# Plain float32 projections as row tiles, and the tails' products as column tiles, in an attention and feed-forward kernel on one core

## The chip, the core and the metric

The kernel runs on one core of a Trainium2 chip. The core has a matrix engine (PE; its weight loads are listed apart as PEld), a vector engine (DVE), a scalar engine (ACT), a general engine (POOL) and a queue that issues transfers (SP). The metric is the device time of one execution in microseconds (us). The time shown for a kernel is the median of several runs.

## What is computed

```
def phi(x):
    proj = x @ w_phi                                   # [64] -> [128]
    proj = proj - max(abs(proj), axis=-1, keepdims)
    return concat([exp(proj), exp(-proj)])             # 256 features
q_p, k_p = phi(q), phi(k)                              # 8 batches, 8 heads, 576 rows
kv  = k_p.T @ v ;  z = sum(k_p, rows)
x   = (q_p @ kv) / (q_p @ z + 1e-6)                    # heads side by side: 512 columns
h   = x.T @ U @ V ;  u = x + h.T                       # mixing over the 576 rows, rank 32
out = u + relu(u @ w_ch1) @ w_ch2                      # 512 -> 2048 -> 512
```

q, k, v and w_phi are float32; U, V and the two large weights come as 64-bit floats and are turned into 32-bit ones by the kernel.

## The kernel before, in words

Heads are worked on in pairs: 8 batches of 4 pairs, 32 in all (class `Pair`). Of the 576 rows of a head 512 are the main part, and the last 64 of both heads of a pair are handled together as the "tail". A pair goes through stages: `transposes`, `s_project_k0`, `s_project_k1`, `s_project_q0`, `s_kv0_q1`, `s_kv1`, `s_out0`, `s_out1`. Between two stages `pace.step()` puts a piece of the feed-forward part (class `Mixer`: `hidden`, L636, and `add`, L657) of the batch before. While one pair (`cur`) gives its outputs, the next (`nxt`) is projected, and the one after that (`far`) is loaded and transposed. When all attention is done, the feed-forward part of what is left follows alone. A scheduler then sets the order of each engine's instructions; each engine runs its own in order.

Two number formats matter. A plain float32 matmul is as exact as the data. A float32r matmul takes numbers of fewer bits; to keep the result exact the kernel splits a number into a high and a low part (`hi`, `lo`) and adds several products. The feed-forward part does so everywhere (three products for one).

The projections by w_phi (64 rows deep, while the array has 128) are done in two ways:

- Batches 0 and 1 (`split` is false): q and k are transposed by PE (L328), and the projections are plain float32 (L389 for K, L432 for Q) against `w_two`, a weight tile in which the two heads' copies of w_phi stand in a block diagonal, so that half of the product is by zeros.
- Batches 2 to 7 (`split` is true): q and k come in by 16 transfers a pair and are transposed by DVE in place (L320). ACT then writes the high parts into one half of the 128 rows of `T` (L323), and DVE the low parts into the other half (L324). So one float32r matmul of 128 rows multiplies high and low parts at once. K takes 8 matmuls of 256 columns a pair (L404), against `w_hl`, which holds the high and the low part of w_phi side by side; ACT copies one half of the result (L407) and DVE adds the other (L408). Q takes 4 matmuls of 512 columns (L427, L428).

The tails are projected in L378/L379 and L416/L417 (L381 and L419 in batches 0 and 1). The products of the features, `kv_main` (L450) and `out_main` (L491), are plain float32 and divided into two column tiles: each matmul has 64 output partitions, and two neighbours use the two halves of the array. The tails' part of kv (L441) and of the output (L477) use the whole array. In L477 both heads' kv stand side by side, and half of the product is not used.

PSUM has 8 banks here: 3 for attention and small products ("at"), 1 for the hidden layer ("ph") and 4 for its output ("o"). In batch 0 some attention tiles use "o". In the first 88 us 37 matmuls on zeros (L763, `keep_busy`) fill PE.

Of the kernel before, what the change touches and what calls it, by code (L numbers as in the profile page):

```python
# [21 lines left out]
P = 128  # L22
# [3 lines left out]
def tile_kernel(  # L26
# [60 lines left out]
    w_hl = const.tile([P, 2, F], F32R, name="w_hl")  # L87
    w_hi, w_lo = w_hl[:, 0, :], w_hl[:, 1, :]
    w_two = const.tile([P, 2, F], F32, name="w_two")

    def load_w_phi():

        for g in range(2):
            nc.sync.dma_start(out=w_f[g * D:(g + 1) * D, :], in_=w_phi)
        nc.gpsimd.memset(w_two, 0.0)
        for g in range(2):
            r_ = slice(g * D, (g + 1) * D)
            nc.vector.tensor_copy(out=w_two[r_, g, :], in_=w_f[r_, :])
        nc.vector.tensor_copy(out=w_hi, in_=w_f)
        nc.vector.tensor_sub(w_lo, w_f, f32(w_hi))  # L100
# [153 lines left out]
    class Pair:  # L254


        def __init__(self, b, j):
# [5 lines left out]
            for n, src in enumerate((k, q)):  # L263
                m = raw.tile([P, 2, SM // 2], F32, tag="raw", bufs=2, name=f"raw{nm}_{n}")
# [34 lines left out]
        def stack(self, src, dst):  # L299

            nc.scalar.copy(out=dst[0:D], in_=src)
            nc.vector.tensor_sub(dst[D:2 * D], src, f32(dst[0:D]))

        def transposes(self):
# [6 lines left out]
            dt = F32R if self.split else F32  # L311
            self.tail_T = att.tile([P, 2, P], dt, tag="tail_T", name=f"tail_T{nm}")
            if not self.split:
                nc.gpsimd.memset(self.tail_T, 0.0)
            self.T = []
            for n in range(2):
                if self.split:
                    m = att.tile([P, 2, SM], F32R, tag=f"T{n}", name=f"T{n}_{nm}")
                    x_ = self.raw[n].rearrange("p h e -> p (h e)")
                    nc.vector.transpose(out=x_, in_=x_)  # L320
                    for s in range(2):
                        here, there = (slice(i * D, (i + 1) * D) for i in (s, 1 - s))
                        nc.scalar.copy(out=m[here, s, :], in_=x_[here])  # L323
                        nc.vector.tensor_sub(m[there, s, :], x_[here], f32(m[here, s, :]))  # L324
                else:
                    pT = self.ps(f"T{n}_", True)
                    for c in range(NT):
                        nc.tensor.transpose(  # L328
                            out=pT[:, c * P:(c + 1) * P],
                            in_=self.raw[n][:, c // 2, c % 2 * P:(c % 2 + 1) * P],  # L330
                            identity=ident)
                    m = att.tile([P, SM], F32, tag=f"T{n}", name=f"T{n}_{nm}")
                    nc.scalar.copy(out=m, in_=pT)
# [3 lines left out]
                for g in range(2):  # L337
                    r_ = slice(g * D, (g + 1) * D)
                    tv = tT[r_, 0:2 * ST].rearrange("p (n r) -> p n r", n=2)
                    if self.split:  # L340
                        self.stack(tv, self.tail_T[:, :, r_])
                    else:
                        nc.scalar.copy(out=self.tail_T[r_, :, r_], in_=tv)

        def k_tile(self, n, ng):
            tag, bufs = ("feat", 3) if ng > 1 else ("feat_t", 2)
# [16 lines left out]
        def q_features(self, n, pq, m):  # L363
            nm = f"{self.nm}_{n}"
            tag, bufs = ("feat", 3) if m == SM else ("feat_t", 2)
            qp = att.tile([P, 2, m], F32, tag=tag, bufs=bufs, name=f"qp{nm}")
            nc.scalar.copy(out=qp[:, 1, :], in_=pq[:, 0:m])  # L367
# [6 lines left out]
        def project_k_tail(self):  # L374
            pk = self.ps("pkt")
            kT = self.tail_T[:, 0, :]
            if self.split:
                nc.tensor.matmul(pk[:, 0:F], kT, w_hi, start=True, stop=False)  # L378
                nc.tensor.matmul(pk[:, 0:F], kT, w_lo, start=False, stop=True)  # L379
            else:  # L380
                nc.tensor.matmul(pk[:, 0:F], kT, w_f, start=True, stop=True)  # L381
            self.kpt = self.k_features("t", pk[:, 0:F].unsqueeze(1), self.k_tile("t", 1))

        def project_k(self, g):
            if self.split:
                return self.project_k_split(g)
            pk = self.ps(f"pk{g}_", True)
            for s in range(2):
                nc.tensor.matmul(  # L389
                    pk[:, s * 2 * F:(s + 1) * 2 * F],  # L390
                    self.T[0][:, (2 * g + s) * P:(2 * g + s + 1) * P],
                    w_two.rearrange("p g f -> p (g f)"), start=True, stop=True)
            return self.k_features(
                g, pk.rearrange("p (t f) -> p t f", f=F), self.k_tile(g, NT))

        def project_k_split(self, g):

            kp = self.k_tile(g, NT)
            k_w = kp[:, :, F:2 * F]
            for s in range(2):  # L400
                pk = self.ps(f"pk{g}{s}_").rearrange("p (t n f) -> p t n f", t=2, n=2)
                for i in range(2):
                    cs = slice((2 * g + s) * P, (2 * g + s + 1) * P)
                    nc.tensor.matmul(  # L404
                        pk[:, i, :, :], self.T[0][:, i, cs], w_hl, start=True, stop=True)
                ts_ = slice(s, NT, 2)
                nc.scalar.copy(out=kp[:, ts_, 0:F], in_=pk[:, :, 1, :])  # L407
                nc.vector.tensor_tensor(  # L408
                    out=k_w[:, ts_, :], in0=pk[:, :, 0, :], in1=kp[:, ts_, 0:F], op=ALU.add)
            return self.k_features(g, k_w, kp)  # L410

        def project_q_tail(self):
            pq = self.ps("pqt")
            qT = self.tail_T[:, 1, :]
            if self.split:
                nc.tensor.matmul(pq[:, 0:2 * ST], w_hi, qT, start=True, stop=False)  # L416
                nc.tensor.matmul(pq[:, 0:2 * ST], w_lo, qT, start=False, stop=True)  # L417
            else:
                nc.tensor.matmul(pq[:, 0:2 * ST], w_f, qT, start=True, stop=True)  # L419
            self.qpt = self.q_features("t", pq, 2 * ST)  # L420

        def project_q(self, s):

            pq = self.ps(f"pq{s}_")
            if self.split:
                qT = self.T[1][:, s, :]
                nc.tensor.matmul(pq, w_hi, qT, start=True, stop=False)  # L427
                nc.tensor.matmul(pq, w_lo, qT, start=False, stop=True)  # L428
            else:
                pv = pq.rearrange("f (p z i) -> f i z p", z=2, i=2)  # L430
                for i in range(2):
                    nc.tensor.matmul(  # L432
                        pv[:, i], w_two[:, i, :],
                        self.T[1][:, s * (SM // 2):(s + 1) * (SM // 2)], start=True, stop=True)
            return self.q_features(s, pq, SM)

        def kv_tail(self):
            self.kv_ps = self.ps("kv_ps", True)
            self.kv_v = self.kv_ps[:, 0:4 * (D + 1)].rearrange("p (f h e) -> p f h e", f=2, h=2)
            for f in range(2):  # L440
                nc.tensor.matmul(  # L441
                    self.kv_v[:, f, :, :], self.kpt[:, 0, f * F:(f + 1) * F], self.vt,
                    start=(f == 0), stop=False, skip_group_check=True)

        def kv_main(self, g, kp):
            for t in range(NT):
                for f in range(2):
                    for i in range(2):
                        r_ = slice(i * H, (i + 1) * H)
                        nc.tensor.matmul(  # L450
                            self.kv_v[r_, f, g, :], kp[:, t, f * F + i * H:f * F + (i + 1) * H],
                            self.vb[:, g, t, :], start=False, stop=(t == NT - 1),
# [18 lines left out]
        def out_tail(self, xt):  # L471
# [4 lines left out]
            for f in range(2):  # L476
                nc.tensor.matmul(  # L477
# [476 lines left out]
```

## Time and profile before

| | |
|---|---|
| median of 3 runs | 1177.5 us (1177.25 to 1177.62) |
| profiled execution, its own time | 1175.22 us |
| its span | 1173.4 us |
| granted PE clock, mean | 0.999 |
| last projection of batch 1 (L432), start | 180.1 us |
| last projection of all (L427), start | 942.5 us |
| matmuls of the hidden layer and its output (L636, L657) | 3456 of 512 columns |
| transfers, mean | 86 GB/s |

A row of a group reads: line, engine, operation, output <- inputs, shape, count, then busy time in us, mean length of one in ns, the idle time of the engine just before them and what ended it. Matmuls are pipelined: one of 512 columns is listed with some 390 ns, but the next one starts earlier. So the distance between starts is what one costs, and a row of the view in order of time (start, length, line, tile, count) gives it for a run of equal ones: the whole length less the length of the last, divided by the count less one. A plain float32 matmul appears as two records, a float32r one and a transpose as one.

### The profile page before, as it was taken

To read this page: it belongs to the slowest core of one execution; us is meant where nothing else is said; L and a number is where in the kernel's file an instruction comes from. 1 tells how busy PE (TensorE), PEld (TensorE's weight loads), DVE (VectorE), ACT (ScalarE), POOL (GpSimd) and SP (SyncE) were. 2 spreads that over 40 slices of the span, in tenths; PEclk is the share of its full clock that TensorE was granted. 3 is DMA by queue.
4 is the path that set the end of the run, shared out by engine and by line. 5 is a ranking of instruction groups with operands and counts; after the bars stand their busy time and mean duration, and the time that the engine had idled before them with its cause. 6 is when DMAs were issued, how large, how long until landed. Compare 5 with 4: busy or idle time off the path is not lost.

```text
span 1173.4 us, 22343 instructions
## 1 busy us (share of the span) xinstructions
PE 1146.9 (98%) x8717; PEld 933.6 (80%) x8717; DVE 677.2 (58%) x1482; ACT 536.0 (46%) x1151; POOL 203.2 (17%) x154
## 2 busy tenths in 40 slices
PE   7989999999999999999999999999999999999998
PEld 5767877788888888788887888788878887888886
DVE  5677779766647666766657565756666533312111
ACT  5778787545534544354534444444534421111110
POOL 3344444111111121012101111112101110000000
PEclk9999999999999999999999999999999999999999
DMA  4785221421245123531353123512343026310101
GB/s 119 236 290 188 94 64 32 136 74 32 68 112 125 28 57 82 120 77 29 74 130 103 32 67 103 114 42 57 83 92 101 1 73 160 96 37 11 62 1 37
DMA packets 248307, 100.87 MB, mean 86 GB/s; under 512 B 215305, under 2 KB 227849, under 8 KB 248201
## 3 DMA queue, kind: packets, MB, share of 16 engines
q1 hardware_dynamic: 246928, 98.16, 32.0%
q8 instruction: 69, 1.13, 0.4%
q10 hardware_dynamic: 1272, 1.28, 0.4%
q14 instruction: 38, 0.30, 0.1%
HBM read 78.41 MB, written 20.97 MB: 85 GB/s over the span
## 4 chain that ended last, share of the span: by engine, by line
PE 77%; DVE 7%; DMA 5%; SPq 5%; ACT 5%; issue 1%; POOL 0%; DVEq 0%; ACTq 0%; POOLq 0%
PE ph L636 28%; PE o L657 27%; PE kv_ps L450 5%; PE xp L491 5%; SPq L622 3%; PE pk L404 2%; DMA raw<-in_q_dram 2%; PE pq L427 2%; PE pp L572 2%; SPq L270 1%; PE kv_ps L441 1%; DVE x L591 1%; DMA y<-u_dram 1%; PE xpt L477 1%; PE pq L428 1%
## 5 line engine op out<-in xcount | busy, mean ns | idle before, releaser
L636 PE MATMUL ph<-uT_hi,w 128*128 128x512 f32 x1152 | 390.3, 398 | 2.7 <-DVE h_lo L642 1.7
L657 PE MATMUL o<-w,h_hi 128*128 128x512 f32 x1152 | 321.6, 395 | 3.0 <-ACT h_hi L641 2.8
L636 PEld LDWEIGHTS ph<-uT_hi,w 128*128 128x128 f32 x1152 | 215.7, 188 | 51.2 <-DVE h_lo L642 3.3
L657 PEld LDWEIGHTS o<-w,h_hi 128*128 128x128 f32 x1152 | 211.6, 188 | 47.0 <-ACT h_hi L641 4.6
L636 PE MATMUL ph<-uT_lo,w 128*128 128x512 f32 x576 | 225.6, 392 | 0.0
L641 ACT ACTIVATE h_hi<-ph 128x512 fp32r<-128x512 f32 x144 | 85.8, 595 | 285.7 <-PE ph L636 274.6
L642 DVE SCALAR_TENSOR_TENSOR h_lo<-ph,h_hi 128x512 fp32r<-128x512 f32 x144 | 98.8, 686 | 186.9 <-ACT h_hi L641 186.3
L657 PE MATMUL o<-w,h_lo 128*128 128x512 f32 x576 | 188.4, 395 | 0.8 <-DVE h_lo L642 0.7
L368 POOL PARTITION_ALL_REDUCE qp<-qp x64 | 126.5, 1979 | 267.0 <-ACT qp L367 257.6
L657 PEld LDWEIGHTS o<-w,h_lo 128*128 128x128 f32 x576 | 105.8, 188 | 23.5 <-DVE h_lo L642 2.4
L636 PEld LDWEIGHTS ph<-uT_lo,w 128*128 128x128 f32 x576 | 108.3, 188 | 20.2 <-DVE uT_lo L249 0.2
L368 POOL PARTITION_ALL_REDUCE qp_t<-qp_t x32 | 27.4, 856 | 396.3 <-ACT qp_t L367 396.2
L450 PEld LDWEIGHTS kv_ps<-vb,kp 128*64 128x64 f32 x2048 | 69.4, 137 | 22.3 <-issue 13.5
L358 ACT ACTIVATE kp<-kp 128x512 f32<-128x512 f32 x64 | 40.4, 631 | 93.6 <-DVE kp L355 82.8
L491 PEld LDWEIGHTS xp<-kv,qp 128*64 128x64 f32 x2048 | 65.8, 137 | 21.4 <-issue 8.7
L324 DVE TENSOR_TENSOR T<-raw,T 64x512 fp32r<-64x512 f32 x96 | 69.7, 726 | 22.5 <-ACT T L323 19.9
L450 PE MATMUL kv_ps<-vb,kp 128*64 128x65 f32 x2048 | 82.4, 226 | 0.1
L491 PE MATMUL xp<-kv,qp 128*64 128x65 f32 x2048 | 76.1, 225 | 0.8 <-ACT qp L370 0.4
L323 ACT CAST T<-raw 64x512 fp32r<-64x512 f32 x96 | 59.4, 619 | 19.1 <-PE pq L428 17.8
L370 ACT ACTIVATE qp<-qp 128x512 f32<-128x512 f32 x64 | 40.4, 631 | 59.0 <-DVE qp L369 58.8
L320 DVE STREAM_TRANSPOSE raw<-raw 128x512 f32<-128x512 f32 x48 | 34.1, 711 | 55.5 <-DMA raw<-in_q_dram 29.6
L145 POOL INT64_ADD w_ab<-w_ab x32 | 43.5, 1359 | 64.2 <-DVE w_ab L141 43.6
(125 smaller groups left out, 1335.2 us busy)
## 6 DMA issues: line engine op xcount, KB each, us to landing
words<-in_moe_w_ch_dram SPq DMA_DIRECT2D x32, 512.0 KB, 8.7
w<-kept SPq DMA_DIRECT2D x30, 512.0 KB, 4.0
vb<-in_v_dram SPq DMA_DIRECT2D x64, 128.0 KB, 2.7
u_dram<-x SPq DMA_DIRECT2D x32, 256.0 KB, 2.1
st<-u_dram SPq DMA_DIRECT2D x16, 512.0 KB, 3.8
out_dram<-st SPq DMA_DIRECT2D x32, 256.0 KB, 2.3
y<-u_dram SPq DMA_DIRECT2D x112, 64.0 KB, 2.2
raw<-in_k_dram SPq DMA_DIRECT2D x192, 32.0 KB, 1.8
```

The costliest lines, as they stand in the source:

```text
L145: nc.gpsimd.int64_add(a64, a64, b64)
L323: nc.scalar.copy(out=m[here, s, :], in_=x_[here])
L324: nc.vector.tensor_sub(m[there, s, :], x_[here], f32(m[here, s, :]))
L358: nc.scalar.activation(out=kp[:, :, 0:F], in_=kp[:, :, F:2 * F], func=AF.Exp)
L368: nc.gpsimd.partition_all_reduce(qp[:, 0, :], qp[:, 1, :], P, ReduceOp.absmax)
L370: nc.scalar.activation(out=qp[:, 0, :], in_=qp[:, 1, :], func=AF.Exp)
L450: nc.tensor.matmul(self.kv_v[r_, f, g, :], kp[:, t, f * F + i * H:f * F + (i + 1) * H], self.vb[:, g, t, :], start=False, stop=(t == NT - ...
L491: nc.tensor.matmul(xv[i * H:(i + 1) * H, c, :], qp[:, f, c * P + i * H:c * P + (i + 1) * H], self.kv[:, f, c // 2 if self.split else s, :] ...
L636: nc.tensor.matmul(ph, w1_part(f, l, c), r[:, c, :], start=(n == 0), stop=(n == 3 * NCC - 1))
L641: on_act = nc.scalar.activation(out=h_hi, in_=ph, func=AF.Relu)
L642: on_dve = nc.vector.scalar_tensor_tensor(out=h_lo, in0=ph, scalar=0.0, in1=f32(h_hi), op0=ALU.max, op1=ALU.subtract)
L657: ins = nc.tensor.matmul(self.o[t], l[:, cs], w2_t[f][:, r, :], start=(f == 0 and n == 0), stop=(f == NFC - 1 and n == 2))
```

## The change

All projections become plain float32, and the difference between batches 0/1 and 2 to 7 is left to the way in which q and k are transposed. `w_two`, `w_hl` and the high and low parts of q and k are gone; the transposed tile is used as it is. Its upper 64 rows hold one head (batches 0 and 1) or one half of the rows (batches 2 to 7), its lower 64 the other. Each half is multiplied with its own copy of w_phi in the same half of `w_f`, in a matmul of 64 rows: two row tiles of the array, whose results go to two banks. `project_k` and `project_q` do both halves at once, in one stage each; `s_kv0_q1` no longer projects. The tail of K is projected one stage later. The tails' parts of kv and of the output are divided into two column tiles of 64 output partitions, as the main parts are. There is one `tail_T`, zeroed once. The raw tiles have five buffers and take the place of `T`; the features have four instead of three.

```diff
-    w_hl = const.tile([P, 2, F], F32R, name="w_hl")
-    w_two = const.tile([P, 2, F], F32, name="w_two")
+    tail_T = const.tile([P, 2, P], F32, name="tail_T")
+    nc.gpsimd.memset(tail_T, 0.0)
...
-                m = raw.tile([P, 2, SM // 2], F32, tag="raw", bufs=2, name=f"raw{nm}_{n}")
+                m = raw.tile([P, 2, SM // 2], F32, tag="raw", bufs=5, name=f"raw{nm}_{n}")
...
-                    m = att.tile([P, 2, SM], F32R, tag=f"T{n}", name=f"T{n}_{nm}")
-                    x_ = self.raw[n].rearrange("p h e -> p (h e)")
-                    nc.vector.transpose(out=x_, in_=x_)
-                    for s in range(2):
-                        here, there = (slice(i * D, (i + 1) * D) for i in (s, 1 - s))
-                        nc.scalar.copy(out=m[here, s, :], in_=x_[here])
-                        nc.vector.tensor_sub(m[there, s, :], x_[here], f32(m[here, s, :]))
+                    m = self.raw[n].rearrange("p h e -> p (h e)")
+                    nc.vector.transpose(out=m, in_=m)
...
-                    if self.split:
-                        self.stack(tv, self.tail_T[:, :, r_])
-                    else:
-                        nc.scalar.copy(out=self.tail_T[r_, :, r_], in_=tv)
+                    nc.scalar.copy(out=tail_T[r_, :, r_], in_=tv)
...
-        def q_features(self, n, pq, m):
+        def q_features(self, n, parts, m):
...
-            nc.scalar.copy(out=qp[:, 1, :], in_=pq[:, 0:m])
+            for i, part in enumerate(parts):
+                to = qp[:, 1, :]
+                if len(parts) > 1:
+                    to = to.rearrange("f (p z i) -> f i z p", z=2, i=2)[:, i]
+                nc.scalar.copy(out=to, in_=part)
...
+        def project_k(self):
+
+            pk = [self.ps(f"pk{i}_", True) for i in range(2)]
+            for c in range(NT):
+                for i in range(2):
+                    r_ = slice(i * D, (i + 1) * D)
+                    nc.tensor.matmul(
+                        pk[i][:, c * F:(c + 1) * F], self.T[0][r_, c * P:(c + 1) * P], w_f[r_],
+                        start=True, stop=True)
+            self.kp = [
+                self.k_features(
+                    i, pk[i].rearrange("p (t f) -> p t f", f=F), self.k_tile(i, NT))
+                for i in range(2)]
...
+        def project_q(self):
+
+            pq = [self.ps(f"pq{i}_") for i in range(2)]
+            for i in range(2):
+                r_ = slice(i * D, (i + 1) * D)
+                nc.tensor.matmul(pq[i], w_f[r_], self.T[1][r_, :], start=True, stop=True)
...
             for f in range(2):
-                nc.tensor.matmul(
-                    self.kv_v[:, f, :, :], self.kpt[:, 0, f * F:(f + 1) * F], self.vt,
-                    start=(f == 0), stop=False, skip_group_check=True)
...
+                for i in range(2):
+                    r_ = slice(i * H, (i + 1) * H)
+                    nc.tensor.matmul(
+                        self.kv_v[r_, f, :, :], self.kpt[:, 0, f * F + i * H:f * F + (i + 1) * H],
+                        self.vt, start=(f == 0), stop=False, skip_group_check=True)
...
             for f in range(2):
-                nc.tensor.matmul(
-                    xv, self.qpt[:, f, :], self.kv[:, f, :, :], start=(f == 0), stop=(f == 1))
+                for g in range(2):
+                    r_ = slice(g * ST, (g + 1) * ST)
+                    nc.tensor.matmul(
+                        xv[r_, g, :], self.qpt[:, f, r_], self.kv[:, f, g, :],
+                        start=(f == 0), stop=(f == 1))
...
         def s_project_k0(self):
+            self.project_k()
+
+        def s_project_k1(self):
             self.project_k_tail()
-            self.kp0 = self.project_k(0)
...
         def s_project_q0(self):
-            self.qp0 = self.project_q(0)
+            self.project_q()
 
         def s_kv0_q1(self):
             self.kv_tail()
-            self.kv_main(0, self.kp0)
-            self.qp1 = self.project_q(1)
+            self.kv_main(0, self.kp[0])
```

How this stands in PE's order is shown at two places. Names carry batch and pair (`pk00_5_0` is of batch 5, pair 0) and buffer numbers; `ph` and `o` are the feed-forward part. The first place is the K projection of batch 5, pair 0. PE before:

```order
L636 MATMUL ph3_9_6554<-uT_hi3_5483,w1_9_1929 128x512
L378 MATMUL pkt5_0_6596<-w_hl_88,tail_T5_0_6479 128x128
L379 MATMUL pkt5_0_6596<-w_hl_88,tail_T5_0_6479 128x128
L404 MATMUL pk00_5_0_6606<-w_hl_88,T0_5_0_6480 128x256 x2
L657 MATMUL o3_0_5882<-w2_8_3_5898,h_hi3_8_6471 128x512 x2
L657 MATMUL o3_0_5882<-w2_8_3_5898,h_lo3_8_6472 128x512
L657 MATMUL o3_1_5883<-w2_8_3_5898,h_hi3_8_6471 128x512 x2
L404 MATMUL pk01_5_0_6611<-w_hl_88,T0_5_0_6480 128x256 x2
```

PE now, at the same place (L596 and L617 are the hidden layer and its output in the new numbering, `pk0` the upper row tile and `pk1` the lower):

```order
L596 MATMUL ph3_9_6306<-uT_hi3_5304,w1_9_1969 128x512
L365 MATMUL pk0_5_0_6348<-w_f_87,raw5_0_0_6055 128x128
L365 MATMUL pk1_5_0_6349<-w_f_87,raw5_0_0_6055 128x128
L365 MATMUL pk0_5_0_6348<-w_f_87,raw5_0_0_6055 128x128
L365 MATMUL pk1_5_0_6349<-w_f_87,raw5_0_0_6055 128x128
L365 MATMUL pk0_5_0_6348<-w_f_87,raw5_0_0_6055 128x128
L365 MATMUL pk1_5_0_6349<-w_f_87,raw5_0_0_6055 128x128
L365 MATMUL pk0_5_0_6348<-w_f_87,raw5_0_0_6055 128x128
L365 MATMUL pk1_5_0_6349<-w_f_87,raw5_0_0_6055 128x128
L617 MATMUL o3_0_5680<-w2_8_3_5696,h_hi3_8_6243 128x512 x2
```

The four blocks of two whole-array matmuls (two of them shown) have become one block of eight row tiles, upper and lower in turn. The second place is the output of the tail (`xpt`) of batch 4, pair 3. PE before:

```order
L657 MATMUL o3_3_5885<-w2_9_1978,h_hi3_9_6567 128x512 x2
L477 MATMUL xpt4_3_6635<-kv4_3_6552,qp4_3_t_6393 128x130 x2
L636 MATMUL ph3_10_6667<-uT_hi3_5483,w1_10_2005 128x512
L636 MATMUL ph3_10_6667<-uT_lo3_5484,w1_10_2005 128x512
L636 MATMUL ph3_10_6667<-uT_hi3_5483,w1_10_2005 128x512
L491 MATMUL xp0_4_3_6646<-kv4_3_6552,qp4_3_0_6452 64x65 x16
```

PE now:

```order
L617 MATMUL o3_3_5683<-w2_9_2011,h_lo3_9_6320 128x512
L438 MATMUL xpt4_3_6384<-kv4_3_6304,qp4_3_t_6158 64x65 x4
L617 MATMUL o3_0_5680<-w2_9_2011,h_hi3_9_6319 128x512
L596 MATMUL ph3_10_6418<-uT_hi3_5304,w1_10_2038 128x512
L596 MATMUL ph3_10_6418<-uT_lo3_5305,w1_10_2038 128x512
L596 MATMUL ph3_10_6418<-uT_hi3_5304,w1_10_2038 128x512 x2
```

Two whole-array matmuls have become four column tiles, which stand alone between whole-array matmuls; the next column tiles of this pair (`xp0`) follow nine matmuls later in the new order.

More of the change, by code (lines that the diff above doesn't have):

```diff
@@ L94, in load_w_phi @@
             nc.sync.dma_start(out=w_f[g * D:(g + 1) * D, :], in_=w_phi)
[L95 to L100, printed above, removed]
     vts, vbs = [], []
@@ L297, in load_v @@
                     out=self.vt[g * D:(g + 1) * D, g, 0:D], in_=v[self.b, self.h0 + g, SM:S, :])
-        def stack(self, src, dst):
-            nc.scalar.copy(out=dst[0:D], in_=src)
-            nc.vector.tensor_sub(dst[D:2 * D], src, f32(dst[0:D]))
         def transposes(self):
@@ L310, in transposes @@
             nc.tensor.transpose(out=tT[:, 0:2 * ST], in_=self.t_r, identity=ident)
[L311 to L314, printed above, removed]
             self.T = []
@@ L331, in transposes @@
                             identity=ident)
-                    m = att.tile([P, SM], F32, tag=f"T{n}", name=f"T{n}_{nm}")
+                    m = raw.tile([P, SM], F32, tag="raw", bufs=5, name=f"T{n}_{nm}")
                     nc.scalar.copy(out=m, in_=pT)
@@ L375, in project_k_tail @@
             pk = self.ps("pkt")
-            kT = self.tail_T[:, 0, :]
+            nc.tensor.matmul(pk[:, 0:F], tail_T[:, 0, :], w_f, start=True, stop=True)
+            self.kpt = self.k_features("t", pk[:, 0:F].unsqueeze(1), self.k_tile("t", 1))
+        def project_k(self):
[10 more added lines that the diff above has]
+                for i in range(2)]
@@ L377, in project_k_tail, with project_q_tail @@
+        def project_q_tail(self):
+            pq = self.ps("pqt")[:, 0:2 * ST]
+            nc.tensor.matmul(pq, w_f, tail_T[:, 1, :], start=True, stop=True)
+            self.qpt = self.q_features("t", [pq], 2 * ST)
+        def project_q(self):
[3 more added lines that the diff above has]
+                nc.tensor.matmul(pq[i], w_f[r_], self.T[1][r_, :], start=True, stop=True)
             if self.split:
-                nc.tensor.matmul(pk[:, 0:F], kT, w_hi, start=True, stop=False)
@@ L379, in project_k_tail @@
-                nc.tensor.matmul(pk[:, 0:F], kT, w_lo, start=False, stop=True)
-            else:
[L381 to L435, printed above, removed]
+                parts = [[a] for a in pq]
+            else:
+                parts = [
+                    [a[:, g * 2 * P:(g + 1) * 2 * P].rearrange("f (z p) -> f z p", z=2) for a in pq]
+                    for g in range(2)]
@@ L437, in kv_tail @@
+            self.qp = [self.q_features(i, parts[i], SM) for i in range(2)]
         def kv_tail(self):
@@ L440, in kv_tail, with kv_main @@
             for f in range(2):
-                nc.tensor.matmul(
-                    self.kv_v[:, f, :, :], self.kpt[:, 0, f * F:(f + 1) * F], self.vt,
-                    start=(f == 0), stop=False, skip_group_check=True)
-        def kv_main(self, g, kp):
-            for t in range(NT):
+                for i in range(2):
[3 more added lines that the diff above has]
+                        self.vt, start=(f == 0), stop=False, skip_group_check=True)
+        def kv_main(self, n, kp):
+            for c in range(NT):
+                g, z = divmod(c, 2)
+                t = 2 * n + z if self.split else 2 * z + n
                 for f in range(2):
@@ L450, in kv_main @@
                         nc.tensor.matmul(
-                            self.kv_v[r_, f, g, :], kp[:, t, f * F + i * H:f * F + (i + 1) * H],
-                            self.vb[:, g, t, :], start=False, stop=(t == NT - 1),
+                            self.kv_v[r_, f, g, :], kp[:, c, f * F + i * H:f * F + (i + 1) * H],
+                            self.vb[:, g, t, :], start=False, stop=(n == 1 and z == 1),
                             skip_group_check=True)
```

14 lines of the change are left out of this document (5 added, 9 removed).

## The prediction

> **What bounds the kernel now.** First the shares of the page, then the stretches (busy us of each engine, then clock and DMA), then what TensorE waited for (total us, times, longest).
>
> ```profile
> PE 1146.9 (98%) x8717; PEld 933.6 (80%) x8717; DVE 677.2 (58%) x1482; ACT 536.0 (46%) x1151; POOL 203.2 (17%) x154
> ...
> 0.00:100.00 100.00, 86.69 (x938) 65.78 (x939) 68.58 (x177) 71.28 (x158) 38.81 (x47) 1.00 0.72 230
> 100.00:200.00 100.00, 97.13 (x745) 78.60 (x744) 78.54 (x156) 83.65 (x163) 48.56 (x34) 1.00 0.26 70
> 200.00:950.00 750.00, 744.77 (x6029) 609.83 (x6029) 477.62 (x1062) 351.57 (x779) 115.82 (x74) 1.00 0.32 77
> ...
> PE o L657 <- ACT h_hi L641: 2.8, 4, 1.0
> ...
> PE ph L636 <- DVE h_lo L642: 1.7, 3, 0.9
> ```
>
> From 200 to 950 us PE is busy 744.77 of 750 us at a clock of 1.00, while DVE and ACT are busy 64% and 47%. PE's longest waits for them in the whole span are 2.8 and 1.7 us. A busy PE need not be a PE at its peak, because matmuls overlap; so I price it by the distance between starts. The next rows are PE's order of time (start, length, line, tile, count).
>
> ```profile
> 607.97 0.64 PE L404 MATMUL pk<-w_hl,T 128*128 128x256 f32 x4
> 608.44 0.61 PE L477 MATMUL xpt<-kv,qp_t 128*128 128x130 f32 x4
> 608.81 2.08 PE L657 MATMUL o<-w,h_hi 128*128 128x512 f32 x8
> ...
> 613.44 0.61 PE L657 MATMUL o<-w,h_lo 128*128 128x512 f32 x2
> 613.99 1.15 PE L491 MATMUL xp<-kv,qp 128*64 128x65 f32 x32
> 615.07 0.73 PE L657 MATMUL o<-w,h_lo 128*128 128x512 f32 x2
> 615.64 0.64 PE L404 MATMUL pk<-w_hl,T 128*128 128x256 f32 x4
> ...
> L404 PE MATMUL pk<-w_hl,T 128*128 128x256 f32 x192 | 36.4, 291 | 0.4 <-DVE kp L408 0.4
> L427 PE MATMUL pq<-T,w_hl 128*128 128x512 f32 x48 | 23.7, 493 | 0.0
> L428 PE MATMUL pq<-T,w_hl 128*128 128x512 f32 x48 | 19.0, 396 | 0.0
> L477 PE MATMUL xpt<-kv,qp_t 128*128 128x130 f32 x128 | 19.6, 275 | 0.0
> L491 PE MATMUL xp<-kv,qp 128*64 128x65 f32 x2048 | 76.1, 225 | 0.8 <-ACT qp L370 0.4
> ```
>
> Two L657 in 0.61 us, one lasting 0.39, start 0.22 to 0.23 us apart: 0.227 for 512 columns of float32r. A 256-column one takes 0.12 (four in 0.64, the last 0.28). A plain float32 matmul shows as two records (L477: 128 records of 64 matmuls), of 0.112 each for 130 columns. The 32 records of L491, two column tiles side by side, need 0.93 us from first to last start, in 15 steps of two: 0.059 a step, but 0.10 for the first. So **plain float32 costs four times a float32r pass, and tiles side by side halve that**.
>
> The second reading is **what a change of tiling costs**. Between the starts of L657 at 613.44 and L404 at 615.64 lie 2.20 us. Four L657 take 0.91 and 16 steps of 0.059 take 0.94; 0.35 us are left. Going in, the first L491 starts 0.09 later than a 512-column matmul needs (0.32 behind the second L657 of 613.44), and its first step is 0.05 too long. Coming out, L657 starts 0.09 late (0.15 behind the last L491), and the next one 0.11 late (0.73 - 0.39 = 0.34 apart). The weight loads say why.
>
> ```profile
> 652.73 0.19 PEld L636 LDWEIGHTS ph<-uT_hi,w 128*128 128x128 f32 x1
> 652.95 0.39 PE L636 MATMUL ph<-uT_hi,w 128*128 128x512 f32 x1
> 653.27 1.01 PEld L491 LDWEIGHTS xp<-kv,qp 128*64 128x64 f32 x32 [0.35 <-issue]
> 653.27 1.15 PE L491 MATMUL xp<-kv,qp 128*64 128x65 f32 x32
> 654.35 0.19 PEld L427 LDWEIGHTS pq<-T,w_hl 128*128 128x128 f32 x1
> ```
>
> Within one tiling the load runs 0.22 ahead of its matmul. At the change it waits until the last matmul is out and then lies open: 0.05 us for 64 columns, 0.11 for 128. I take 0.14 us for a change into column tiles and 0.207 for one back to the whole array. The Trainium skill (TensorEngine Tiling (Array Packing), Key Properties) says that changing the tiling mode drains the TensorE; these rows agree for column tiles, and nothing here shows row tiles. By that rule the row tiles below pay as the column tiles do.
>
> **The change part by part.** Batches 2 to 7 have 24 head pairs, batches 0 and 1 have 8. "Late" is what lies behind the last projection of batch 1 (180 us here), "early" what lies before.
>
> ```profile
> 164.17 1.03 PE L389 MATMUL pk<-w_two,T 128*128 128x256 f32 x4
> ...
> 170.90 1.02 PE L432 MATMUL pq<-T,w_two 128*128 128x256 f32 x4
> ...
> 604.11 0.22 PE L378 MATMUL pkt<-w_hl,tail_T 128*128 128x128 f32 x1
> 604.17 0.28 PE L379 MATMUL pkt<-w_hl,tail_T 128*128 128x128 f32 x1
> 604.28 0.45 PE L636 MATMUL ph<-uT_hi,w 128*128 128x512 f32 x1
> 604.57 0.39 PE L636 MATMUL ph<-uT_lo,w 128*128 128x512 f32 x1
> ```
>
> - *K, late.* Out: 192 x 0.12 = 23.0 us. In: 192 plain float32 row tiles of 128 columns, 384 records, 192 steps of two. A step is not in the trace. Side by side it is near one record of L477, 0.112 to 0.12; one after the other it is 0.224. I take 0.115, since column tiles do run two at a time: 22.1. In the new order five of the 24 blocks are cut after an odd matmul, and the two at the cut run alone (+0.23 a block). Together +0.2.
> - *Q, late.* Out: 96 x 0.23 = 22.1. In: two row tiles of 512 columns a pair. L389 shows 0.216 a record for 256 columns (1.03 less 0.38, over 3), so 0.432 for 512 and 0.864 for the two steps; 24 times is 20.7 (41.4 one after the other). -1.4.
> - *K and Q of batches 0 and 1.* L389 and L432 are 128 records of 0.216: 27.6 us. In: 8 pairs x (0.92 + 0.864) = 14.3, and five Q pairs that the new order separates cost 0.864 more each, 4.3. -9.
> - *Tails.* k and q tails were two float32r matmuls each and become one plain float32: from 604.11 to 604.57 lie 0.46, of which L636 explains 0.227, so 0.23 as before against 2 x 0.112. Nothing. The tails' output goes from four records of 0.112 to four steps of 0.059: -0.21 x 24 late (-5.1), -1.7 early. The tails' kv part does equal work, with some cut pairs: +1.9 late.
> - *Changes of tiling.* Counted over PE's whole order, from one matmul to the next, there are 334 before and 464 now. Late, before: 121 in, 121 out, 121 x 0.347 = 42.0 us. Now 136 into columns x 0.14, 155 back to the whole array x 0.207 and 53 into rows x 0.20 (0.09 of drain and a 128-column load of 0.11): 61.8. **+19.8 late.** Row tiles are not in the trace; the nearest rows are those of the column tiles, and I let both pay alike. Early 46 x 0.347 = 16.0 becomes 47 x 0.14 + 51 x 0.207 + 22 x 0.20 = 21.5: +5.5. Row tiles bounded from both sides: if their changes are free, late has 136 x 0.347 = 47.2 (+5.2) and early 16.3; if both loads lie open one behind the other, 53 x 0.11 more, +5.8.
> - *DVE and ACT.* They lose the groups below. PE waits so little for them that I count 2 us as gained, at most the 5.2 us that PE stood idle from 200 to 950.
>
> ```profile
> L324 DVE TENSOR_TENSOR T<-raw,T 64x512 fp32r<-64x512 f32 x96 | 69.7, 726 | 22.5 <-ACT T L323 19.9
> L408 DVE TENSOR_TENSOR kp<-pk,kp 128x256 f32<-128x256 f32 x96 | 37.6, 409 | 9.2 <-ACT kp L407 9.1
> L323 ACT CAST T<-raw 64x512 fp32r<-64x512 f32 x96 | 59.4, 619 | 19.1 <-PE pq L428 17.8
> L407 ACT COPY kp<-pk 128x256 f32<-128x256 f32 x96 | 33.1, 371 | 28.8 <-PE pk L404 28.4
> ```
>
> - *Banks and buffers.* A K or Q projection now takes two of the three attention banks at once instead of one. What would wait behind it on PE is the next attention matmul and, in order, everything else. With DVE and ACT lighter I cost it at nothing; a wait of 0.2 us in each of 24 pairs would be 5 us. Five "raw" buffers replace two raw and two T buffers; the loads start no later.
>
> Sum: late 0.2 - 1.4 - 5.1 + 1.9 + 19.8 = +15.4. Early -9 - 1.7 + 5.5 = -5.2; but PE is busy only 86.69 of the first 100 us, so part of that becomes waiting, and I take -3. With -2 for shorter waits: **+10.4 us**. The profiled execution took 1175.22 us (span 1173.4), so 1185.6; the median of the runs lies 2.3 higher, 1177.5, hence **1188 us**.
>
> **The rivals.**
> 1. *Row tiles change over without a drain* (faster). The loads of rows 0 to 63 might be placed while a whole-array matmul runs out. For it: the trace shows the drain for column tiles only. Late then costs 5.2 in place of 19.8 and early 0.3 in place of 5.5. From +10.4 go 20, of which some 2 are lost in early waiting: -7.6, 1170. It decides the sign from about half of that: when a row change costs under 0.1 us.
> 2. *Row tiles share a weight path.* K changes its weights for every 128 columns. If two 128-column loads (0.11 each) go one after the other, a step is 0.22 and not 0.115: 256 steps x 0.105 = +27 us, 1215. Against it: 64-column loads of two column tiles do fit into a step of 0.059. The Trainium skill (TensorE: Matmul & The Clock Gate, Measured speedup vs the span model) has four row tiles gain 3.07 and not 4; as an estimate from that page, two tiles at 77% make the 57 us of projections 74, so 1205.
> 3. *The row tiles do not run side by side at all*, so the change does not do what it says. Late +41.6, early +10: 1240. Column tiles running two at a time speak against it.
>
> **How the numbers follow.** Forecast 0.52 (1180 to 1196), rival 1 0.25, rival 2 0.14, rival 3 0.09. The range leaves out rival 3 and thin ends: 1166 to 1217. A measurement tells 0.2% from no change, 2.4 us: rival 1 gives 0.21 faster and 0.03 same, the forecast 0.03 faster, 0.09 same and 0.40 slower, the others slower. That is 0.24, 0.12, 0.64. The forecast's own range stands beside it because both signs have weight.
>
> **What would show it.** In the new trace a K block between two whole-array matmuls should take 0.92 us beside 0.40 of changing; the starts of its records should come in twos 0.115 us apart. A Q block should take 0.86, twos 0.43 apart. The first weight load of a block should lie 0.09 us behind the drained matmul. Starts evenly 0.11 apart (16 of them, 1.8 us) mean rival 3; twos 0.22 apart rival 2; a row block that begins with no gap rival 1. DVE should lose some 120 us and ACT some 90 with no gain in the span. What would make the forecast wrong elsewhere: PE idle that names a projection bank, or many more us of PE idle between 50 and 100 us than the 13 us that the first 100 us show.

## The result, and the profile after

The changed kernel takes **1198.2 us** (median of 4 runs, 1197.4 to 1200.29) against 1177.55 us of before on the same chip. The ratio is 1.0179, with a 95% interval of 1.0161 to 1.0196: slower by about 21 us. The prediction said slower, 1188 us, with a range from 1166 to 1217. The sign holds, but the loss is twice the +10.4 us of the forecast, and 1198.2 lies above the 1180 to 1196 that the prediction gave for the forecast itself. The profiled execution took 1200.29 us, its span 1198.5.

The first row is the share of each engine on the page of after. DVE lost 106 us and ACT 77, and the span grew.

```profile
PE 1162.2 (97%) x9197; PEld 907.4 (76%) x9197; DVE 571.6 (48%) x1238; ACT 459.1 (38%) x975; POOL 200.9 (17%) x146
```

The stretches of after (start and end, length, then busy us of PE, PEld, DVE, ACT and POOL, then the granted clock, the DMA share and GB/s):

```profile
0.00:100.00 100.00, 81.92 (x938) 55.84 (x939) 60.68 (x160) 70.09 (x160) 35.76 (x39) 0.97 0.67 210
100.00:200.00 100.00, 97.49 (x819) 75.74 (x821) 75.26 (x150) 82.68 (x161) 47.35 (x33) 0.97 0.34 94
200.00:950.00 750.00, 740.34 (x6189) 576.77 (x6187) 372.93 (x815) 267.72 (x586) 113.22 (x72) 1.00 0.32 75
```

PE stood idle for 9.7 us between 200 and 950 where before had 5.2, and for 18.1 us in the first 100 where before had 13.3. The clock, 1.00 in the same three stretches of before, is 0.97 in the first two. What PE waited for in after (total us, times, longest):

```profile
PE o L617 <- ACT h_hi L601: 6.7, 5, 2.4
PE pkt L356 <- DMA w_f<-in_w_phi_dram: 5.5, 1, 5.5
...
PE pq L383 <- DVE kp_t L331: 1.9, 1, 1.9
...
PE T L307 <- ACT qp L347: 1.8, 1, 1.8
PE T L307 <- DVE kp L331: 1.7, 1, 1.7
```

L617 is before's L657, the output of the hidden layer. Its wait for ACT was 2.8 us in four pieces in before, the longest 1.0 us.

Now the row tiles themselves, in after's order of time, a K block and a Q block late in the kernel:

```profile
687.41 0.39 PE L596 MATMUL ph<-uT_hi,w 128*128 128x512 f32 x1
687.72 0.97 PEld L365 LDWEIGHTS pk<-w_f,raw 64*128 64x128 f32 x16 [0.35 <-issue]
687.72 1.16 PE L365 MATMUL pk<-w_f,raw 64*128 64x128 f32 x16
...
688.82 0.45 PE L438 MATMUL xpt<-kv,qp_t 128*64 128x65 f32 x8
...
702.96 1.13 PE L383 MATMUL pq<-raw,w_f 64*128 64x512 f32 x4
...
704.02 0.19 PEld L596 LDWEIGHTS ph<-uT_lo,w 128*128 128x128 f32 x1 [0.76 <-issue]
```

From 687.41 to 688.82 lie 1.41 us. L596 needs 0.227 of them; the 16 records start in twos, and 8 steps of 0.112 need 0.90; 0.28 is left for changing: the 0.20 going in, of drain and open load, and the 0.09 of drain coming out. The first weight load starts with the first matmul, 0.31 behind the L596 ahead of it, so 0.09 after that one is out. The Q block takes 1.06 us to the next load: two steps of 0.43, and 0.20 for its own open load and the drain coming out. **The row tiles run side by side, and a change into them costs what the forecast took.** The rivals are out: no free change, no step of 0.22, no 16 single steps. And the whole order of after has 464 changes of tiling, as counted; priced at 0.14, 0.20 and 0.207 they make 83.1 us against 57.9 for the 334 of before, +25.2 where the forecast had 19.8 + 5.5.

So the error is not in the matmuls. It is in two other terms, the waits and the early stage. The experiments divide the loss.

### The profile page after: what moved, and what is told of

The parts are those of the page before. It is cut to its first block, busy times and chain, and to the rows that moved or that the text cites. A ratio compares the mean times of both kernels' runs of the same rounds, so it can differ in the third digit from the quotient of the medians.

```text
span 1198.5 us, 22826 instructions
## 1 busy us (share of the span) xinstructions
PE 1162.2 (97%) x9197; PEld 907.4 (76%) x9197; DVE 571.6 (48%) x1238; ACT 459.1 (38%) x975; POOL 200.9 (17%) x146
## 4 chain that ended last, share of the span: by engine, by line
PE 80%; DMA 5%; SPq 4%; DVE 4%; ACT 4%; issue 2%; POOL 0%; ACTq 0%; DVEq 0%; POOLq 0%
PE ph L596 30%; PE o L617 29%; PE kv_ps L409 5%; PE xp L453 5%; PE pq L383 3%; PE pk L365 2%; SPq L582 2%; SPq L263 2%; PE kv_ps L398 2%; PE pp L532 2%; DMA u_dram<-x 1%; DMA v_st<-in_moe_V_dram 1%; PE vp L550 1%; DMA y<-u_dram 1%; ACT uT_hi L241 1%
## 5 line engine op out<-in xcount | busy, mean ns | idle before, releaser
L596 PE MATMUL ph<-uT_hi,w 128*128 128x512 f32 x1152 | 389.2, 399 | 1.9 <-DVE h_lo L602 1.2
L617 PE MATMUL o<-w,h_hi 128*128 128x512 f32 x1152 | 354.0, 399 | 6.7 <-ACT h_hi L601 6.7
L596 PEld LDWEIGHTS ph<-uT_hi,w 128*128 128x128 f32 x1152 | 216.4, 188 | 60.5 <-DVE x L428 7.6
L617 PEld LDWEIGHTS o<-w,h_hi 128*128 128x128 f32 x1152 | 212.5, 189 | 58.1 <-ACT h_hi L601 8.8
L596 PE MATMUL ph<-uT_lo,w 128*128 128x512 f32 x576 | 226.2, 393 | 0.2
L617 PE MATMUL o<-w,h_lo 128*128 128x512 f32 x576 | 215.0, 397 | 0.3 <-DVE h_lo L602 0.3
L596 PEld LDWEIGHTS ph<-uT_lo,w 128*128 128x128 f32 x576 | 108.7, 189 | 26.0 <-issue 4.5
L617 PEld LDWEIGHTS o<-w,h_lo 128*128 128x128 f32 x576 | 108.2, 189 | 26.0 <-issue 2.3
L453 PEld LDWEIGHTS xp<-kv,qp 128*64 128x64 f32 x2048 | 66.1, 137 | 26.1 <-issue 17.1
L409 PE MATMUL kv_ps<-vb,kp 128*64 128x65 f32 x2048 | 77.5, 224 | 0.0
L334 ACT ACTIVATE kp<-kp 128x512 f32<-128x512 f32 x64 | 39.4, 631 | 96.3 <-DVE kp L331 96.1
L349 DVE TENSOR_TENSOR qp<-qp 128x512 f32<-128x512 f32 x64 | 60.5, 946 | 19.0 <-POOL qp L348 18.5
L347 ACT COPY qp<-pq 128x512 f32<-128x512 f32 (+1 forms) x80 | 44.5, 612 | 51.6 <-PE pq L383 51.5
```

The costliest lines, as they stand in the source:

```text
L334: nc.scalar.activation(out=kp[:, :, 0:F], in_=kp[:, :, F:2 * F], func=AF.Exp)
L347: nc.scalar.copy(out=to, in_=part)
L349: nc.vector.tensor_sub(qp[:, 1, :], qp[:, 1, :], qp[:, 0, :])
L409: nc.tensor.matmul(self.kv_v[r_, f, g, :], kp[:, c, f * F + i * H:f * F + (i + 1) * H], self.vb[:, g, t, :], start=False, stop=(n == 1 and ...
L453: nc.tensor.matmul(xv[i * H:(i + 1) * H, c, :], qp[:, f, c * P + i * H:c * P + (i + 1) * H], self.kv[:, f, c // 2 if self.split else s, :] ...
L596: nc.tensor.matmul(ph, w1_part(f, l, c), r[:, c, :], start=(n == 0), stop=(n == 3 * NCC - 1))
```

## The experiments

All times below are medians, with the ratio to before measured beside them (and its 95% interval), since before itself moved between 1176.6 and 1178.7. "Counted" means work and changes of tiling, priced as in the prediction over the kernel's whole order.

**Each half of the change alone.** tails_only is before with the tails' kv part and outputs in column tiles, and nothing else of the change:

```diff
...
-                nc.tensor.matmul(
-                    xv, self.qpt[:, f, :], self.kv[:, f, :, :], start=(f == 0), stop=(f == 1))
+                for g in range(2):
+                    r_ = slice(g * ST, (g + 1) * ST)
+                    nc.tensor.matmul(
+                        xv[r_, g, :], self.qpt[:, f, r_], self.kv[:, f, g, :],
+                        start=(f == 0), stop=(f == 1))
```

> The kernel of before with only the tails' kv part and output as column tiles. Theory A (each change of tiling costs PE 0.14 us into column tiles and 0.207 back, on the path): PE's order has 390 changes instead of 334, 56 x 0.174 = +9.7 us, and 5.9 us less work, so 1177.5 + 3.8 = 1181. Theory B (changes of tiling cost little; the unforeseen part of the time is PE waiting for ACT, DVE or transfers, and the half clock that follows such a wait): only the lighter work counts, 1172.

Measured: 1198.0 us, 1.0177 [1.0157, 1.0197]. Both expectations missed: this small part alone costs as much as the whole change, with 3.8 us counted.

rows_late has row tiles in batches 2 to 7 alone, with the tails' products on the whole array as in before:

```diff
+            self.rows = self.split
...
+            if self.rows:
+                self.kp0, self.kp1 = self.rows_k()
+                return
...
```

> Before, but with plain float32 row tiles in batches 2 to 7 only; batches 0 and 1 and the tails' whole-array products as before. Theory A: 410 changes instead of 334, 73.7 us of them instead of 57.9 (+15.8), and 1.0 us less work: 1177.5 + 14.7 = 1192. Theory B: the first 180 us are as before, so the waits and the half clock there do not come, and the rest costs nothing: about 1180.

Measured: 1195.8 us, 1.0159 [1.0135, 1.0183], a few us above theory A and far from B. The two parts do not add up (20.8 and 18.7 us alone, 21 together), so at least one of them costs something alone that it does not cost within the whole change, and that is not a change of tiling.

**More changes of tiling.** after_cutk is after with the K tail's whole-array matmul put into the middle of each K block:

```diff
+                if c == 2:
+                    pt = self.ps("pkt")
+                    tc.keep_in_program_order(nc.tensor.matmul(
+                        pt[:, 0:F], tail_T[:, 0, :], w_f, start=True, stop=True))
...
```

> The changed kernel with the price of a change of tiling doubled at one place: the whole-array matmul of K's tail is put into the middle of each K block, so that the block is cut in two. Same work. PE's order has 539 changes instead of 464, priced at 98.3 us instead of 83.1 (+15.2), with 1.2 us less for tiles that stand alone. Theory A: 1198.2 + 14 = 1212. Theory B: 1198 to 1201. If row changes were free and only column changes priced: 1199 to 1204.

Measured: 1214.1 us, 1.0309 [1.0294, 1.0324], 15.3 us above after by the ratios, good to some 3 us. The 75 added changes were counted at 15.2, with 1.2 less for tiles that no longer stand alone. The price of a change of tiling therefore holds in the time, not only in the rows.

**The wait for h_hi.** In after's trace PE's longest idle stretch behind the start is this one:

```profile
629.01 1.23 ACT L334 ACTIVATE kp<-kp 128x512 f32<-128x512 f32 x2 [7.40 <-DVE kp L331]
...
630.15 1.13 ACT L335 ACTIVATE kp<-kp 128x512 f32<-128x512 f32 x2
...
631.08 0.39 PE L375 MATMUL pqt<-tail_T,w_f 128*128 128x128 f32 x2
631.19 2.16 ACT L241 CAST uT_hi<-y 128x512 fp32r<-128x512 f32 x4
...
633.25 0.58 ACT L601 ACTIVATE h_hi<-ph 128x512 fp32r<-128x512 f32 x1
...
633.89 1.02 PE L617 MATMUL o<-w,h_hi 128*128 128x512 f32 x3 [2.43 <-ACT h_hi L601]
```

At the end of a batch ACT casts the four uT_hi blocks of the next batch, 2.16 us in a row, and the cast of the last hidden block, for which PE waits, stands behind them in ACT's queue. Ahead of them stand four activations of K features (two of L334, two of L335), since `project_k` now hands both halves of K on at once. From 629.01 to 633.25 that is 4.24 us of work ahead of the awaited cast. At the same batch end of before it was 2.75 us, of two activations and three casts:

```profile
613.62 0.63 ACT L358 ACTIVATE kp<-kp 128x512 f32<-128x512 f32 x1 [4.57 <-DVE kp L355]
...
614.28 0.63 ACT L359 ACTIVATE kp<-kp 128x512 f32<-128x512 f32 x1
614.82 1.64 ACT L248 CAST uT_hi<-y 128x512 fp32r<-128x512 f32 x3
...
616.37 0.58 ACT L641 ACTIVATE h_hi<-ph 128x512 fp32r<-128x512 f32 x1
...
617.01 0.73 PE L657 MATMUL o<-w,h_hi 128*128 128x512 f32 x2 [0.73 <-ACT h_hi L641]
```

after_hfirst turns the order of the casts round: two more chunks of the hidden layer go ahead of the blocks, and these are issued after that cast. The activations stay where they are.

```diff
+            self.last = on_act.ins
...
-            mix(len(todo) - HELD)
+            mix(len(todo) - HELD + 2)
+            last = todo[0][0].__self__.last
             for c in range(NCC):
-                m.turn_blocks(c)
-                mix(c % 2)
+                with tc.issue_after(last):
+                    m.turn_blocks(c)
```

> The changed kernel, but at the end of each batch ACT casts the last hidden block (h_hi) before the four blocks of the next batch's input (uT_hi), which stood ahead of it; changes of tiling 460 instead of 464. In the trace of the changed kernel PE stood 0.7 to 2.7 us at six such places, 8 us in all, and lost some 1.7 us more to a half clock after the longest. If these waits are part of the unforeseen 10 us: 1198.2 - 6 to - 9 = 1189 to 1192, with no half clock near 635 us. If PE merely waits later for the next batch's input: 1196 to 1199.

Measured: 1189.6 us, 1.0095 [1.0076, 1.0114], as expected: 9.9 us less than after by the ratios. The same place in its trace:

```profile
629.22 0.58 ACT L601 ACTIVATE h_hi<-ph 128x512 fp32r<-128x512 f32 x1
629.70 0.61 ACT L241 CAST uT_hi<-y 128x512 fp32r<-128x512 f32 x1
...
629.85 0.50 PE L618 MATMUL o<-w,h_hi 128*128 128x512 f32 x1 [0.56 <-ACT h_hi L601]
```

**The same edit on the other kernels.** before has a like order on ACT, with gaps of about 1 us, so the edit was made there and in the partial kernels too.

> Before with the last chunk's h_hi cast ahead of the four blocks of the next batch on ACT, as in after_hfirst; its matmuls and its 334 changes of tiling stay. Before has five gaps of 0.8 to 1.3 us at the batch ends, where after has 0.7 to 2.7. Theory A (the batch-end wait costs before about 3 us and after about 9): 1174 to 1175 us. Rival B (those gaps hide another limit of before): 1177 to 1179. If A holds, the version of after with this edit (1189.6) is about 15 us slower than its own before, and that is the change without the batch-end wait: 25 us of changes of tiling less about 12 us of matmul work.

Measured: 1173.8 us, 0.9963 [0.9945, 0.9981]. Theory A holds. before loses 4.4 us at its batch ends and after 9.9. This is also the fastest kernel of the study, faster than both.

> rows_late with the same edit. By its order 400 changes of tiling, some of them into rows (+14.0 us over before_hfirst), and 1.6 us less matmul work, +12.4 in all. Its only long gaps were at 160 us and at the batch ends (7.1 us of h_hi waits). Theory A: 12 us above before_hfirst, 1186 to 1188. Rival B (other waits take the place of the one removed): 1192 to 1196. A is likelier.

Measured: 1186.1 us, 1.0074 [1.0059, 1.0089], 13 us above before_hfirst by the ratios, where 12.4 were counted. With the batch-end wait gone, the late row tiles cost what their work and changes of tiling were counted to cost, within the error of some 3 us.

> after_hfirst without column tiles in the tails: row tiles in all batches, whole-array tails. By its order 433 changes of tiling (-3.8 us against after_hfirst) and 6.0 us more matmul work: +2.2. Theory A (the counted sums decide): 1190 to 1193, so the tails' column tiles inside the whole change are worth about 2 us. Rival B (alone, they cost 20 us, and most of that comes on top here too): 1175 to 1182.

The edit is the two hunks of tails_only taken back. Measured: 1190.4 us, 1.0110 [1.0095, 1.0125]. That is 1.8 us above after_hfirst, less than the error: the tails' column tiles gain little or nothing within the change (2.2 us were counted), although they cost 20 us when made alone.

> tails_only with the same edit. By its order it has 392 changes of tiling (58 more than before_hfirst, +10.1 us) and 5.9 us less matmul work, +4.2 in all. Theory A (the rest of tails_only's +20 is the batch-end wait): about 4 us above before_hfirst, 1178 to 1180. Rival B (the rest is mostly the early waits with the half clock after them, 158, 205 and 242 us in its trace, which this edit does not touch): 1186 to 1193. I hold B for likelier here: of its 18 us of waiting the batch ends show some 5.

Measured: 1201.8 us, 1.0205 [1.0188, 1.0222], further off than either expectation. Its stretch from 185 to 950 us, in the columns used above:

```profile
185.00:950.00 765.00, 746.58 (x6102) 600.17 (x6103) 482.24 (x1069) 358.58 (x788) 122.35 (x77) 1.00 0.32 75
```

PE is idle for 18.4 us there, where before_hfirst has 4.8 (its stretch follows below), on short waits, most of them for DVE. One of them:

```profile
675.43 0.71 DVE L320 STREAM_TRANSPOSE raw<-raw 128x512 f32<-128x512 f32 x1 [4.00 <-DMA raw<-in_k_dram]
676.06 0.65 DVE L647 SCALAR_TENSOR_TENSOR h_lo<-ph,h_hi 128x512 fp32r<-128x512 f32 x1
...
676.77 0.79 PE L641 MATMUL ph<-uT_hi,w 128*128 128x512 f32 x1 [1.83 <-DVE h_lo L647]
```

DVE stood for 4.00 us at a transpose whose load had not landed; the h_lo that PE needed was next in DVE's queue. Such waits of DVE for loads are not new (79 us in all from 200 to 950, against 64 in before_hfirst, where the longest was 4.4); new is that PE ran out of other work at some of them. So the new order has waits of its own, besides the one that the edit cures.

**The early stage apart.** late_tails_hfirst is rows_late_hfirst with the tails in column tiles: all of the change but its first two batches (and but the fourth buffer of the features).

> rows_late_hfirst (row tiles in batches 2 to 7 alone, five buffers for raw) with the tails in column tiles as well: all of the change but its first two batches. By its order 41 more changes of tiling than rows_late_hfirst (+6.6 us) and 5.6 us less matmul work, +1.0 in all. after_hfirst, which has the first two batches in row tiles too, is 5.1 us less than rows_late_hfirst by the same count, but was measured 3.5 us above it. Theory A (the 8.6 us between those two lie in the first 185 us, where row tiles leave PE idle and the half clock follows): 1186 to 1188, the first 185 us as in before. Rival B (column tiles in the tails bring waits of their own, as tails_only's 20 us might say): 1192 or more, the excess after 185 us.

Measured: 1186.4 us, 1.0061 [1.0046, 1.0076]. Theory A holds. Its stretches beside those of before_hfirst and after_hfirst, in this order:

```profile
25.00:185.00 160.00, 150.31 (x1473) 117.88 (x1469) 116.12 (x261) 127.48 (x256) 70.37 (x48) 0.99 0.53 165
185.00:950.00 765.00, 764.28 (x6454) 597.77 (x6450) 384.60 (x849) 282.27 (x612) 118.38 (x76) 1.00 0.31 75
```

```profile
25.00:185.00 160.00, 153.74 (x1474) 122.30 (x1477) 119.79 (x264) 129.09 (x261) 71.98 (x55) 1.00 0.53 165
185.00:950.00 765.00, 760.24 (x6164) 623.31 (x6164) 493.79 (x1104) 366.46 (x809) 122.38 (x78) 1.00 0.32 76
```

```profile
25.00:185.00 160.00, 151.89 (x1528) 112.59 (x1527) 118.03 (x261) 129.62 (x270) 71.59 (x48) 0.94 0.54 165
185.00:950.00 765.00, 761.61 (x6427) 594.41 (x6426) 387.39 (x846) 282.51 (x612) 119.50 (x76) 1.00 0.32 75
```

Late, PE's idle time is 4.8 us in before_hfirst, 0.7 in late_tails_hfirst and 3.4 in after_hfirst. So a relief of 1 to 4 us is there; whether the lighter DVE and ACT bring it or the five raw buffers was not tried apart. Early, after_hfirst has a clock of 0.94, where the others have 1.00 and 0.99. That is 0.06 x 160 / 0.5, some 19 us at half clock. Early, PE is idle for 9.7 us in late_tails_hfirst and for less, 8.1, in after_hfirst (6.3 in before_hfirst), so it is not the sum of idle time that sets the clock. In these traces the last output matmul of batch 1 ends at 205.2 us in late_tails_hfirst and at 210.1 in after_hfirst.

> before_hfirst with only the tails' outputs in column tiles, and these issued in the middle of the first output block (after its second tile of rows), which is in column tiles already. By its order 26 more changes of tiling (+4.6 us; the scheduler still cuts some blocks apart) and 6.6 us less matmul work, -2.0 in all. Theory A (counted sums decide): 1171 to 1173, so the best of all. Rival B (waits move, as in tails_only): 1176 to 1190.

The edit issues the four column-tile matmuls of the tails' outputs behind `c == 1` in `out_main(0, ...)`. Measured: 1192.2 us, 1.0123 [1.0104, 1.0142], above even rival B's range: some 19 us above before_hfirst, although less was counted than for it. tails_only, tails_hfirst and this one all lose 17 us or more beyond their counts, and by other waits in each: PE's longest group late is for h_lo of DVE in tails_hfirst and for h_hi of ACT here. In all three, 11 to 12 us of the loss lie before the end of batch 1's last output matmul (213.1 to 215.1 us, against 202.7 in before and 202.3 in before_hfirst). late_tails_hfirst, which has the tails of tails_hfirst without the high and low parts on ACT and DVE and with five raw buffers, does not have this loss. Which of these two cures it was not tried apart.

**ACT's copies of Q.** In batches 0 and 1 the upper 64 rows of the transposed tile hold every second token of both heads (not one head, as "The change" has it). A feature tile is of one head, so after copies it out of two banks in two pieces.

```diff
-            if self.split:
-                parts = [[a] for a in pq]
-            else:
-                parts = [
-                    [a[:, g * 2 * P:(g + 1) * 2 * P].rearrange("f (z p) -> f z p", z=2) for a in pq]
-                    for g in range(2)]
-            self.qp = [self.q_features(i, parts[i], SM) for i in range(2)]
+            self.qp = [self.q_features(i, [pq[i]], SM) for i in range(2)]
...
```

> after_hfirst, but in batches 0 and 1 each row tile's Q is taken over whole by one copy of 128x512 (the tokens of one parity of both heads, as batches 2 to 7 do by halves) and not by two of 128x256 per feature tile, one out of each bank. In the first 185 us ACT spent 16.6 us on 30 copies of 128x256 (646 ns) where before_hfirst spent 9.3 us on 16 of 128x512 (582 ns), so about 7 us of ACT goes; the matmuls stay and the order counts 463 changes of tiling (+1.0 with its work). Theory A (the early excess of 9 us over late_tails_hfirst is these copies: PE waits for banks that they empty late, and the half clock follows): 1182 to 1186. Rival B (it is the half clock after waits that have other causes, such as the weights' conversion on ACT and the bank held by kp_t): 1189 to 1191.

With one copy a bank, the tokens of batches 0 and 1 reach x in another order, and the mixing over the rows does not follow them: this kernel does not give the result of the reference, and only its time is of use. The amount of work is the same. Measured: 1193.6 us (1187.29 to 1193.78), 1.0123 [1.0091, 1.0155]. The copies in the first 185 us, of after_hfirst and of this kernel (the last columns are busy us, mean ns, and idle time ahead):

```profile
L347 ACT COPY qp<-pq 128x256 f32<-128x256 f32 x30 | 16.6, 646 | 3.1 <-PE pq L383 3.0
```

```profile
L347 ACT COPY qp<-pq 128x512 f32<-128x512 f32 x14 | 8.1, 577 | 2.3 <-PE pq L383 2.2
```

ACT is rid of some 8 us and the time does not fall; it lies above rival B's range too. Theory A is wrong: the copies are not what the early stage loses.

## Why the prediction was right in sign and half in size

By the ratios, times 1177.5 us, the loss of 21.1 us divides as follows. The first two steps are differences of two ratios, good to some 3 us; the third is made of three ratios, good to some 4.

| step | how measured | us | forecast |
|---|---|---|---|
| late: batches 2 to 7, batch-end wait apart | late_tails_hfirst less before_hfirst | +11.5 | +15.4 - 2 |
| early: batches 0 and 1 | after_hfirst less late_tails_hfirst | +4.0 | -3 |
| batch-end wait | (after less after_hfirst) less (before less before_hfirst) | 9.9 - 4.4 = +5.5 | 0 |

- **What bounds the kernel, the cost of row tiles, the count of changes: right.** Steps of 0.112 for K (forecast 0.115) and 0.43 for Q, 0.20 into rows, +25.2 us for all changes of tiling. after_cutk and rows_late_hfirst show that the time follows this count. The forecast for the late stage was met within the error. The sign rests on this count alone, for the waits and the early stage both came out the other way than forecast. The stated range held by luck: it reached up to 1217 for rival 2, which the rows rule out, and the forecast's own ended at 1196.
- **"With -2 for shorter waits": the step that failed first.** It read PE's waits of before, 2.8 and 1.7 us (sums; the longest single ones were 1.0 and 0.9), as a ceiling that lighter engines can only lower. But what PE waits for is one cast, and that cast waits its turn in ACT's queue. At the batch end shown, the new order has four activations and four uT_hi casts ahead of it, 4.24 us, where before had two and three, 2.75 us; the work taken from ACT (L323, L407) had not stood there. PE's wait there grew from 0.73 to 2.43 us. Over the whole of the profiled executions the wait for h_hi grew by 3.9 us (2.8 to 6.7), and the half clock behind the longest one adds 1.7: together 5.6, against the 5.5 of the table. Turning the order of five ACT instructions round gave back 9.9 us. That moved the casts alone; what the two further activations cost was not tried.
- **"-5.2; ... I take -3": the second.** The early stage came out at +4. What the prediction left out is that an idle PE can lose clock (last section). In the profiled execution of after_hfirst 20.5 us of the early stage run at half clock; PE was busy for 18.7 of them, so it did 9.3 us of full-clock work and lost as much. In that of late_tails_hfirst it is 3.4 us and 1.7. These 7.6 us are the largest part found of what the early stage missed, from one execution each. They do not explain all of it: the counts put after_hfirst 6.1 us below late_tails_hfirst, PE is idle for 1.6 us less, and with 7.6 of clock that gives about 0 and not +4, a rest little above the error. Of the two signs that the prediction named, "many more us of PE idle between 50 and 100 us" did not come (6.0 in after and 4.4 in after_hfirst, 4.75 in before); "PE idle that names a projection bank" did, next point. Taking half of ACT's copying away did not help, and what would is open.
- **"Banks and buffers ... I cost it at nothing"**: of after's waits shown above, the two of T L307 and the one of pq L383 are for a bank that a projection's features still hold. They are 5.4 us of idle PE, all early, and each of the three lies in the window ahead of one of after's early half-clock stretches (last section). Of what else a projection of both halves at once does, the prediction saw nothing: it hands ACT the features of two K blocks in a row, which the batch ends paid for.

## What to carry to other kernels

Price a change of array tiling like an instruction: count it over PE's whole order and multiply, here 0.35 us for a block of column tiles and some 0.40 for one of row tiles, in and out. A wait shown as small is no ceiling for the changed kernel: look at what stands ahead of the awaited instruction in its engine's queue, since a new order decides how much of it PE meets. And a gap of some 2 us in a busy PE can cost more than its length, as the last section shows, so gaps are to be counted against the clock too.

## What the runs showed of the hardware

The clock of TensorE can halve after PE was idle for only part of a short window. In after, pairs of the stretch ahead and the stretch at half clock (PE's busy us come first behind the length, the clock third from the end):

```profile
20.30:23.70 3.40, 1.28 (x8) 1.00 (x9) 2.27 (x6) 2.03 (x5) 0.00 (x0) 1.00 0.56 172
23.70:27.10 3.40, 3.38 (x23) 2.40 (x25) 0.64 (x2) 2.87 (x8) 1.66 (x1) 0.50 0.03 7
81.70:85.10 3.40, 1.62 (x11) 1.31 (x11) 0.87 (x3) 3.39 (x9) 0.73 (x1) 1.00 1.07 377
85.10:88.50 3.40, 3.40 (x13) 2.12 (x10) 1.93 (x4) 1.78 (x5) 3.13 (x2) 0.50 1.09 284
173.90:177.30 3.40, 1.56 (x33) 1.06 (x29) 3.37 (x8) 3.40 (x7) 1.57 (x1) 1.00 0.41 66
177.30:184.10 6.80, 6.73 (x13) 4.29 (x14) 4.88 (x10) 3.86 (x11) 4.25 (x3) 0.50 0.07 12
631.30:634.70 3.40, 0.97 (x5) 0.67 (x4) 2.93 (x7) 2.69 (x6) 0.62 (x1) 0.99 0.00 0
634.70:638.10 3.40, 3.40 (x9) 2.67 (x8) 1.85 (x6) 0.62 (x2) 0.22 (x1) 0.50 0.00 0
```

The half-clock stretches start on one grid: 85.1 - 23.7 is 18 times 3.41, 177.3 - 85.1 is 27 times, 634.7 - 177.3 is 134 times. Over the 13 traces of this study, from 25 to 1150 us, the windows of that grid (3.41 us each) at full clock were sorted by PE's busy share. Under 0.5, 18 of 19 were followed by half clock; from 0.5 to 0.6, 11 of 23; from 0.6 to 0.7, 2 of 34; above, 1 of 4154. So an idle stretch of some 1.7 us can halve the clock of the next 3.4 or 6.8 us, if it falls into one window. rows_late had gaps of 2.3 and 3.1 us between starts that lay across two windows (the emptier one 0.49 and 0.54 busy) and kept its clock. In after the four stretches last 17.1 us, and PE was busy for 16.9 of them, 8.5 us of full-clock work.

The Trainium skill (TensorE: Matmul & The Clock Gate, What's actually happening) gives the window as 4096 cycles at 1.2 GHz, 3413 ns, running free of the kernel; the grid agrees. The same section lets the clock fall after at least one idle window; here it fell after windows in which PE was busy for 0.97 to 1.62 of 3.4 us.
